# Three changes to one attention and mixer kernel: 64x64 float32 products on unpadded tiles, remainders in groups, attention tiles held to a clock

## The chip, the cores and the metric

The kernel runs on one core of one Trainium2 chip. The core has five engines that work through their own instruction lists in order: TensorE (PE in the rows; PEld is its weight load), VectorE (DVE), ScalarE (ACT), GpSimd (POOL) and SyncE (SP), which here only issues DMAs. The metric is the device time of one execution in microseconds; lower is better.

## The reference

```python
def _attn_ref(q, k, v):                     # B, H, S, D = 8, 8, 576, 64; chunks of 64 positions
    scores = scale * np.matmul(q_c, k_c.transpose(0, 1, 2, 4, 3))
    scores = scores - np.max(scores, axis=-1, keepdims=True)
    attn = np.exp(scores)
    attn = attn / (np.sum(attn, axis=-1, keepdims=True) + 1e-09)
    out = np.matmul(attn, v_c)

def _moe_ref(x, w_in, w_spatial, b_spatial, w_out):     # x: (8, 576, 512)
    h = np.maximum(x @ w_in, 0.0)
    u, v = (h[..., :d_ff // 2], h[..., d_ff // 2:])
    ...
    v_n = (v - mu) / np.sqrt(var + 1e-06)
    v_s = np.einsum('ts,bsd->btd', w_spatial, v_n) + b_spatial[None, :, None]
    return ((u * v_s) @ w_out).astype(np.float32)

def _moe2_ref(x, U, V, w_ch1, w_ch2):
    h = x.transpose(0, 2, 1) @ U @ V
    u = x + h.transpose(0, 2, 1)
    ch = np.maximum(u @ w_ch1, 0.0) @ w_ch2
    return (u + ch).astype(np.float32)
```

Attention works inside chunks of 64 positions, so each of the 8 x 8 x 9 chunks is a 64x64 score block of its own. Its output goes through the two mixers.

## The kernel before

**Tiles.** The host lays the attention inputs out as 36 tiles of 128x512: two chunks stacked on the partitions (rows 0 to 63 and 64 to 127), 8 heads of 64 columns. Tiles 0 to 8 belong to batch elements 0 and 1 (nine tiles for two elements; tile 4 holds the last chunk of both), and so on.

**Two ways to do attention.** Tiles 0 to 8 (`gen_first`) are multiplied in float32. A product uses the whole 128x128 array: the two chunks' q stand block-diagonally in a zero-padded 128x128 weight block `qb`, so one product per head gives both chunks' scores `sp` (L516), and likewise `vb` for the outputs `of` (L537). DVE and POOL write the zeros (L445 to L448), a DMA brings q and v to a staging place, and ACT copies the halves to their places (L478, L498); q of tiles 5 to 8 is loaded straight into place by two DMAs each (L487). Between the products are the maximum, subtraction, exponential, sum and division (`a_softmax`, `a_norm`) and a transpose `tp` on PE (L529). Tiles 9 to 35 (`gen_attn`) use three float16 products (`mm3`: high by high, high by low, low by high), for which ACT and POOL split q, k, v and the attention into a high and a low part (L362 to L366, L375, L376, L571, L572), in buffers that are written for each tile anew.

**Mixers.** `gen_moe(b)` does, for batch element b, the products `pb<-w,xT` with a layer norm (L655 to L631), `up` (L678), the spatial product with `sp_m` (L693 to L695, gated on DVE at L697), the product with `w_o`, a transposing DMA `tr`, and the rank-32 update: `u_stage` gives `ast`, `v_stage` multiplies it with `v4` (L746), adds it into `x2` on DVE (L747) and splits the sum into the slice buffer `uT` (ACT L750, POOL L751). The last stage cuts the 8 x 576 positions into 9 slices of 512; so element b's first `512 - 64*b` positions end slice b, and the remaining `64 + 64*b` begin slice b+1, one `v_stage` for each of the four 128-row groups m. `gen_ch(j)` does the two large products on slice j: `phid`, then `hid` (ACT L828, DVE L830), then `acc`, over 16 blocks f.

**Weights.** All weights arrive as float64 bit patterns. Each is converted by ACT (L173), three DVE steps (L180, L181, L184), ACT (L191) and POOL (L192) into a high and a low half. Twelve are needed for the first mixer, and 32 more (two for each f) for `gen_ch(0)`; `want(f)` makes sure that those of f stand ahead of its products. Weights and the q and k of tiles 9 on share three staging buffers (`ld4`).

**Order.** Tiles 0 to 4 come first, together with eight weights; then element 0's mixer, with tiles 5 to 8 and the start of element 1's in its gaps. After that three streams (attention from tile 9, mixers, `gen_ch`) are woven together by `Flow.run`, a planner with a clock of its own in ns: it takes from the first stream, in the order of priority, whose time has come. A scheduler then sets each engine's final order from its own estimate of times, so a change in one place moves instructions elsewhere. PSUM has few buffers: three (`h`) are shared by all `pb` and `phid`, and one (`a`) by the float16 scores, their outputs and the transposes.

```python
            if kind == "pe":
                self.tick(val)
                self.t += val
                best[1] = self.t + val * best[3]
            elif kind == "wait":
                best[1] = max(best[1], self.t + val)
```

Of the kernel before, what the change touches and what calls it, by code (L numbers as in the profile page):

```python
# [36 lines left out]
LDV = (3, 4)  # L37
MEMSET = (0, 1, 0, 1, 1)
# [14 lines left out]
class Flow:  # L53
# [13 lines left out]
    def run(self):  # L67
        while self.streams:
            best = None
            for s in self.streams:  # L70
                if s[2] is not None:
                    if s[2] in self.ev:
                        s[1] = max(s[1], self.ev[s[2]])
                        s[2] = None
                    else:
                        continue
                if s[1] <= self.t:
                    best = s
                    break
            if best is None:  # L80
                t = min(s[1] for s in self.streams if s[2] is None)
                self.t = t
                continue
            try:
                kind, val = next(best[0])
            except StopIteration:
                self.streams.remove(best)
                continue
# [5 lines that stand above are left out]
                best[1] = max(best[1], self.t + val)  # L94
            elif kind == "pace":
                best[3] = val
            elif kind == "need":
                best[2] = val
# [3 lines left out]
def moe_kernel(  # L102
# [46 lines left out]
    def mm3(o, wh, wl, xh, xl, start, stop):  # L149
        nc.tensor.matmul(out=o, lhsT=wh, rhs=xh, start=start, stop=False)  # L150
# [273 lines left out]
    def first_loads():  # L424
# [17 lines left out]
        for i in range(5):  # L442
            z = wf[:, i * 3072:i * 3072 + 2048]
            if i < 1:
                nc.vector.memset(z[:, 0:1024], 0.0)  # L445
                nc.gpsimd.memset(z[:, 1024:2048], 0.0)
            else:
                (nc.gpsimd if MEMSET[i] else nc.vector).memset(z, 0.0)  # L448
# [21 lines left out]
    def first_qk(i):  # L470
        qb, vb, kf, pt = first_bufs(i)
        if i < 5:
            qs = wf[:, 15360 + (i % 2) * 512:15360 + (i % 2 + 1) * 512]
            nc.sync.dma_start(out=qs, in_=q[i])
            nc.sync.dma_start(out=kf, in_=k[i])
            for c in range(2):
                r = slice(c * 64, (c + 1) * 64)
                nc.scalar.copy(out=qb[r, :, c, :], in_=qs[r].rearrange("p (h n) -> p h n", h=H))  # L478
            if i + 1 in FILL:

                z = idle[i + 1] = sb.tile([128, 512], F16, tag=("ph", "kd", "se")[i], name="idle", bufs=1 + (i == 2))
                nc.vector.memset(z, 0.0)
                nc.scalar.activation(out=z[0:1, 0:1], in_=qs[0:1, 0:1], func=ACTF.Copy, scale=0.0)
            return
        for c in range(2):
            r = slice(c * 64, (c + 1) * 64)
            nc.sync.dma_start(out=qb[r, :, c, :], in_=q[i][r].rearrange("p (h n) -> p h n", h=H))  # L487
        nc.sync.dma_start(out=kf, in_=k[i])

    def first_v(i):  # L490
        qb, vb, kf, pt = first_bufs(i)
        vs = pt.rearrange("p a n -> p (a n)")
        if i in LDV:
            vs = sb.tile([128, 512], F32, tag="ldv", name="vs", bufs=1)
        nc.sync.dma_start(out=vs, in_=v[i])
        for c in range(2):
            r = slice(c * 64, (c + 1) * 64)
            nc.scalar.copy(out=vb[r, :, :, c, :], in_=vs[r].rearrange("p (a c e) -> p a c e", a=4, c=2))  # L498

    def first_bufs(i):  # L500
        o = (0, 1, 2, 3, 4, 2, 3, 4, 2)[i] * 3072
        qb = wf[:, o:o + 1024].rearrange("p (h c n) -> p h c n", h=H, c=2)
        vb = wf[:, o + 1024:o + 2048].rearrange("p (a c x e) -> p a c x e", a=4, c=2, x=2)
        kf = wf[:, o + 2048:o + 2560]
        pt = wf[:, o + 2560:o + 3072].rearrange("p (a n) -> p a n", a=4)
        return qb, vb, kf, pt

    def gen_first(lo, hi):

        for i in range(lo, hi):  # L510
# [4 lines left out]
            for h in range(H):  # L515
                nc.tensor.matmul(  # L516
                    out=sp[:, h, :], lhsT=qb[:, h].rearrange("p c n -> p (c n)"), rhs=kf[:, h * 64:(h + 1) * 64],
                    start=True, stop=True,
                )
# [14 lines left out]
            for hp in range(4):  # L534
                for c in range(2):
                    tt = slice(c * 64, (c + 1) * 64)
                    nc.tensor.matmul(  # L537
                        out=o[:, hp, tt], lhsT=vb[:, hp, c].rearrange("p x e -> p (x e)"), rhs=pt[:, hp, tt],
                        start=True, stop=True,
                    )  # L540
# [6 lines left out]
    def gen_attn(lo, hi):  # L547
# [5 lines left out]
        for i in range(lo, hi):  # L553
# [3 lines left out]

            kd = spl.pop(i)
            sp = ps_a.tile([128, H, 64], F32, tag="a", name="sp")
            qm = qbd.rearrange("p a h c t -> p a h (c t)")  # L560
            for h in range(H):
                mm3(sp[:, h, :], qm[:, 0, h, :], qm[:, 1, h, :], kd[:, 0, h, :], kd[:, 1, h, :], True, True)
# [40 lines left out]
    def gen_moe(b):  # L603
# [191 lines left out]
        for m in range(4):  # L795
            v_stage(m, n1, S - n1, b + 1, 0)
            yield "pe", mmcost(S - n1)
# [201 lines left out]
```

## Time and profile before

| | |
|---|---|
| median of 3 runs (lowest, highest) | 1310.97 us (1307.9, 1312.58) |
| the profiled execution's own time | 1309.03 us |
| its span, first to last instruction | 1307.1 us |
| PE busy | 1261.7 us, 97% |
| DVE, ACT, POOL busy | 510.3, 518.2, 512.3 us |
| mean granted TensorE clock | 0.990 |

A busy time is the sum of the stretches in which an engine works. A matmul's end is modelled, and the next one starts before it ends, so PE's busy time says where PE stands still and not how full it is while it works. The profiled execution lies 1.94 us below the median.

### The profile page before, as it was taken

How to read it: one execution, taken by the hardware profiler on the slowest of the kernel's cores; microseconds unless marked ns; L12 is line 12 of the kernel's file. 1: busy time of each engine (PE TensorE's matmuls, PEld its weight loads, DVE VectorE, ACT ScalarE, POOL GpSimd, SP SyncE). 2: the span in 40 equal slices, each digit the busy share in tenths (PEclk: the TensorE clock that was granted, in tenths of full speed). 3: DMA queues.
4: the chain of work that ended last, by engine and by line, in shares of the span. 5: the costliest groups of instructions: out<-in, count | busy, mean ns of one | idle time of the engine just before them, and what ended most of it. 6: DMA issues, size and time to landing. Idle time of an engine off the chain costs nothing.

```text
span 1307.1 us, 20572 instructions
## 1 busy us (share of the span) xinstructions
PE 1261.7 (97%) x8324; PEld 722.9 (55%) x8324; DVE 510.3 (39%) x946; ACT 518.2 (40%) x1062; POOL 512.3 (39%) x644
## 2 busy tenths in 40 slices
PE   7899887899999999999999999999999999999998
PEld 5677455444666556654665456645654565544443
DVE  7965787655333533334233513242113211221211
ACT  7865566545445434534244424323123212221110
POOL 6755877646556444525155415223111311020000
PEclk7899899999999999999999999999999999999999
DMA  7645353532224311321034101300011001000000
GB/s 284 194 134 134 113 170 91 132 90 73 64 63 92 82 25 42 83 43 42 5 74 84 49 1 33 45 33 5 1 28 42 1 1 29 24 18 1 33 1 33
DMA packets 99015, 81.43 MB, mean 62 GB/s; under 512 B 73828, under 2 KB 74468, under 8 KB 98920
## 3 DMA queue, kind: packets, MB, share of 16 engines
q1 hardware_dynamic: 97768, 75.92, 21.8%
q10 hardware_dynamic: 1152, 4.19, 1.0%
q8 instruction: 65, 1.06, 0.3%
q14 instruction: 30, 0.25, 0.1%
HBM read 53.62 MB, written 9.44 MB: 48 GB/s over the span
## 4 chain that ended last, share of the span: by engine, by line
PE 79%; DVE 6%; DMA 4%; ACT 4%; POOL 4%; issue 2%; SPq 0%; DVEq 0%; ACTq 0%; POOLq 0%
PE acc L150 9%; PE acc L152 9%; PE acc L151 9%; PE phid L150 9%; PE phid L151 9%; PE phid L152 9%; PE pb L150 8%; PE pb L151 8%; PE pb L152 8%; DMA st<-in_wk_dram 2%; DVE dt L181 2%; DVE dt L184 2%; POOL wch L192 1%; ACT dt L173 1%; DVE dt L180 1%
## 5 line engine op out<-in xcount | busy, mean ns | idle before, releaser
L830 DVE SCALAR_TENSOR_TENSOR hid<-phid,hid 128x512 f16<-128x512 f32 x144 | 99.1, 690 | 388.3 <-ACT hid L828 388.2
L150 PE MATMUL phid<-uT,wch 128*128 128x512 f16 x576 | 218.8, 380 | 2.3 <-DVE hid L830 2.3
L151 PE MATMUL acc<-hid,wch 128*128 128x512 f16 x576 | 218.3, 379 | 0.8 <-DVE hid L830 0.8
L151 PE MATMUL phid<-uT,wch 128*128 128x512 f16 x576 | 218.6, 380 | 0.0
L152 PE MATMUL phid<-uT,wch 128*128 128x512 f16 x576 | 218.6, 379 | 0.0
L152 PE MATMUL acc<-hid,wch 128*128 128x512 f16 x576 | 218.3, 379 | 0.0
L150 PE MATMUL acc<-hid,wch 128*128 128x512 f16 x576 | 207.0, 379 | 0.5 <-ACT hid L828 0.4
L152 PEld LDWEIGHTS <-wch 128*128 128x128 f16 x1152 | 112.8, 98 | 132.8 <-issue 1.6
L150 PEld LDWEIGHTS <-wch 128*128 128x128 f16 x1152 | 112.8, 98 | 118.2 <-issue 2.4
L151 PEld LDWEIGHTS <-wch 128*128 128x128 f16 x1152 | 112.8, 98 | 117.3 <-issue 3.0
L828 ACT ACTIVATE hid<-phid 128x512 f16<-128x512 f32 x144 | 85.4, 595 | 189.8 <-PE phid L152 189.0
L376 POOL TENSOR_TENSOR vbd<-vf,vbd 64x512 f16<-64x512 f32 x54 | 64.6, 1197 | 112.1 <-ACT vbd L375 105.2
L702 POOL TENSOR_TENSOR gt<-g,gt 128x288 f16<-128x288 f32 x64 | 50.4, 789 | 142.4 <-ACT gt L700 142.1
L363 POOL TENSOR_TENSOR qbd<-qk,qbd 64x512 f16<-64x512 f32 x54 | 63.8, 1181 | 53.4 <-ACT qbd L362 51.4
L768 POOL TENSOR_TENSOR tr<-x,tr 128x64 f16<-128x64 f32 x64 | 46.8, 752 | 92.1 <-issue 50.0
L751 POOL TENSOR_TENSOR uT<-x,uT 128x512 f16<-128x512 f32 (+7 forms) x64 | 47.6, 755 | 89.0 <-ACT uT L750 86.1
L150 PE MATMUL pb<-xT,w 128*128 128x288 f16 x256 | 73.8, 288 | 2.3 <-DVE x L747 1.4
L150 PE MATMUL pb<-sp_m,vn 128*128 128x288 f16 x256 | 73.2, 286 | 2.8 <-DVE g L697 1.7
L150 PE MATMUL pb<-gt,w 128*128 128x288 f16 x256 | 72.9, 286 | 3.0 <-DVE hid L830 2.3
L152 PE MATMUL pb<-xT,w 128*128 128x288 f16 x256 | 73.8, 288 | 0.0
L151 PE MATMUL pb<-xT,w 128*128 128x288 f16 x256 | 73.8, 288 | 0.0
L152 PE MATMUL pb<-sp_m,vn 128*128 128x288 f16 x256 | 73.2, 286 | 0.0
(179 smaller groups left out, 2305.0 us busy)
## 6 DMA issues: line engine op xcount, KB each, us to landing
st<-in_wk_dram SPq DMA_DIRECT2D x24, 512.0 KB, 3.5
out_dram<-ot SPq DMA_DIRECT2D x32, 256.0 KB, 2.1
vf<-in_v_dram SPq DMA_DIRECT2D x27, 256.0 KB, 2.7
qk<-in_q_dram SPq DMA_DIRECT2D x27, 256.0 KB, 2.7
qk<-in_k_dram SPq DMA_DIRECT2D x27, 256.0 KB, 3.0
room<-in_wk_dram SPq DMA_DIRECT2D x8, 512.0 KB, 7.2
wch<-in_wk_dram ACTq DMA_DIRECT2D x8, 512.0 KB, 3.2
wch<-in_k_dram SPq DMA_DIRECT2D x9, 256.0 KB, 4.4
```

The lines of the kernel that those rows point to most:

```text
L150: nc.tensor.matmul(out=o, lhsT=wh, rhs=xh, start=start, stop=False)
L151: nc.tensor.matmul(out=o, lhsT=wh, rhs=xl, start=False, stop=False)
L152: nc.tensor.matmul(out=o, lhsT=wl, rhs=xh, start=False, stop=stop)
L181: nc.vector.scalar_tensor_tensor(out=tb, in0=w[:, 0::2], scalar=29, in1=tb, op0=ALU.logical_shift_right, op1=ALU.bitwise_or)
L184: nc.vector.scalar_tensor_tensor(out=tb, in0=w[:, 1::2], scalar=0x80000000, in1=tb, op0=ALU.bitwise_and, op1=ALU.bitwise_or)
L363: nc.gpsimd.tensor_tensor(out=qbd[r, 1, :, c, :], in0=qv[r], in1=qbd[r, 0, :, c, :], op=ALU.subtract)
L376: nc.gpsimd.tensor_tensor(out=vbd[r, 1, :, :, c, :], in0=vf[r], in1=vbd[r, 0, :, :, c, :], op=ALU.subtract)
L702: nc.gpsimd.tensor_tensor(out=gt[:, 1, m, c], in0=g, in1=gt[:, 0, m, c], op=ALU.subtract)
L751: nc.gpsimd.tensor_tensor(out=buf[:, 1, m, c], in0=x2[:, m, t], in1=buf[:, 0, m, c], op=ALU.subtract)
L768: nc.gpsimd.tensor_tensor(out=th[:, o0:o0 + n], in0=x2[:, m, t0:t0 + n], in1=th[:, t0:t0 + n], op=ALU.subtract)
L828: nc.scalar.activation(out=hd[:, 0, :], in_=p, func=ACTF.Relu)
L830: nc.vector.scalar_tensor_tensor(out=hd[:, 1, :], in0=p, scalar=0.0, in1=hd[:, 0, :], op0=ALU.max, op1=ALU.subtract)
```

## The change

For tiles 0 to 8 the zero padding, the staging and the copies go: q, k and v are loaded once, straight to where they are used, and every product is split in two products of 64x64, one for each chunk, on rows 0 to 63 and 64 to 127. The tiles' places in the buffer are listed in `FIRST_AT_COL`. In the mixer, the remainder `S - n1` of the four groups m is done `g = min(4, 512 // n2)` groups at a time in one PSUM buffer, with one DVE, one ACT and one POOL instruction for all of them. For tiles 9 to 17 the planner gets a new word, `until`: tile i isn't begun before 45000 + 16000 (i - 9) ns of its clock, and the first score product of these tiles is kept where the program puts it.

```diff
+FIRST_AT_COL = (0, 3072, 6144, 9216, 12288, 6144, 9216, 12288, 6144)
...
+            elif kind == "until":
+                best[1] = max(best[1], val)
...
+    def mm3(o, wh, wl, xh, xl, start, stop, pin=False):
+        m = nc.tensor.matmul(out=o, lhsT=wh, rhs=xh, start=start, stop=False)
+        if pin:
+            tc.keep_in_program_order(m)
...
-        for i in range(5):
-            z = wf[:, i * 3072:i * 3072 + 2048]
-            if i < 1:
-                nc.vector.memset(z[:, 0:1024], 0.0)
-                nc.gpsimd.memset(z[:, 1024:2048], 0.0)
-            else:
-                (nc.gpsimd if MEMSET[i] else nc.vector).memset(z, 0.0)
...
     def first_qk(i):
         qb, vb, kf, pt = first_bufs(i)
-        if i < 5:
-            qs = wf[:, 15360 + (i % 2) * 512:15360 + (i % 2 + 1) * 512]
-            nc.sync.dma_start(out=qs, in_=q[i])
-            nc.sync.dma_start(out=kf, in_=k[i])
-            for c in range(2):
-                r = slice(c * 64, (c + 1) * 64)
-                nc.scalar.copy(out=qb[r, :, c, :], in_=qs[r].rearrange("p (h n) -> p h n", h=H))
...
-        for c in range(2):
-            r = slice(c * 64, (c + 1) * 64)
-            nc.sync.dma_start(out=qb[r, :, c, :], in_=q[i][r].rearrange("p (h n) -> p h n", h=H))
+        nc.sync.dma_start(out=qb, in_=q[i])
         nc.sync.dma_start(out=kf, in_=k[i])
...
     def first_v(i):
-        qb, vb, kf, pt = first_bufs(i)
-        vs = pt.rearrange("p a n -> p (a n)")
...
-        nc.sync.dma_start(out=vs, in_=v[i])
-        for c in range(2):
-            r = slice(c * 64, (c + 1) * 64)
-            nc.scalar.copy(out=vb[r, :, :, c, :], in_=vs[r].rearrange("p (a c e) -> p a c e", a=4, c=2))
+        nc.sync.dma_start(out=first_bufs(i)[1], in_=v[i])
...
             for h in range(H):
-                nc.tensor.matmul(
-                    out=sp[:, h, :], lhsT=qb[:, h].rearrange("p c n -> p (c n)"), rhs=kf[:, h * 64:(h + 1) * 64],
-                    start=True, stop=True,
-                )
+                for c in range(2):
+                    r, n = slice(c * 64, (c + 1) * 64), slice(h * 64, (h + 1) * 64)
+                    nc.tensor.matmul(out=sp[r, h, :], lhsT=qb[r, n], rhs=kf[r, n], start=True, stop=True)
...
+                    for x in range(2):
+                        r = slice(x * 64, (x + 1) * 64)
+                        nc.tensor.matmul(
+                            out=o[r, hp, tt], lhsT=vb[r, hp * 128 + c * 64:hp * 128 + (c + 1) * 64], rhs=pt[r, hp, tt],
+                            start=True, stop=True,
+                        )
...
+            if i < 18:
+                yield "until", 45000.0 + 16000.0 * (i - 9)
...
-                mm3(sp[:, h, :], qm[:, 0, h, :], qm[:, 1, h, :], kd[:, 0, h, :], kd[:, 1, h, :], True, True)
+                mm3(sp[:, h, :], qm[:, 0, h, :], qm[:, 1, h, :], kd[:, 0, h, :], kd[:, 1, h, :], True, True,
+                    i < 18 and h == 0)
...
-        for m in range(4):
-            v_stage(m, n1, S - n1, b + 1, 0)
-            yield "pe", mmcost(S - n1)
+        n2 = S - n1
+        g = min(4, 512 // n2)
+        buf = slice_buf(b + 1)
+        for m0 in range(0, 4, g):
+            p = b_psum(b)
+            o = p[:, 0:g * n2].rearrange("p (m t) -> p m t", m=g)
+            for j in range(g):
+                nc.tensor.matmul(out=o[:, j], lhsT=ast[:, m0 + j, :], rhs=v4[:, n1:S], start=True, stop=True)
+            ms = slice(m0, m0 + g)
+            t = x2[:, ms, n1:S]
+            nc.vector.scalar_tensor_tensor(
+                out=t, in0=o, scalar=float(2 ** -14), in1=t, op0=ALU.mult, op1=ALU.add
+            )
+            nc.scalar.copy(out=buf[:, 0, ms, 0:n2], in_=t)
+            nc.gpsimd.tensor_tensor(out=buf[:, 1, ms, 0:n2], in0=t, in1=buf[:, 0, ms, 0:n2], op=ALU.subtract)
+            yield "pe", mmcost(n2, g)
```

The lines of the changed kernel are numbered a few lower or higher than before; in the excerpts below L494 is what L516 was, L504 what L529 was, L514 what L537 was, L183, L184 and L187 what L180, L181 and L184 were, L599 what L618 was, and L786 is the new DVE step of a grouped remainder.

First, PE's order right after the 16 fill products that stand ahead of tile 1's scores. `sp` are scores, `tp` transposes, `of` outputs of the float32 tiles, `pb<-w,xT` the first mixer. Before:

```order
L516 MATMUL sp<-wch 128x64 x8
L529 MATMUL tp<-ident,wch 128x128 x4
L537 MATMUL of<-wch 128x64 x8
L516 MATMUL sp<-wch 128x64 x8
L150 LDWEIGHTS xT
L150 MATMUL pb<-w_75,xT 128x512
```

and of the change:

```order
L494 MATMUL sp<-wch 64x64 x48
L504 MATMUL tp<-ident,wch 128x128 x4
L514 MATMUL of<-wch 64x64 x16
L151 LDWEIGHTS xT
L151 MATMUL pb<-w_75,xT 128x512
```

The scores of tiles 1, 2 and 3 now stand in one piece ahead of tile 0's transposes; before, it was tile 1's alone.

Second, DVE's order at the end of element 0's mixer, where the remainder of 64 positions is added into `x2`; `rz` and `mv` belong to element 1's layer norm, `dt` to weights. Before:

```order
L618 TENSOR_SCALAR rz_1427<-rz_1427,mv_1431,y_1434 128x512
L657 BN_AGGR mv_1488<-bs_1486 128x2
L181 SCALAR_TENSOR_TENSOR dt_1503<-st_1501,dt_1503 128x512
L747 SCALAR_TENSOR_TENSOR x2_1029<-pb_1557,x2_1029 128x64
L747 SCALAR_TENSOR_TENSOR x2_1029<-pb_1562,x2_1029 128x64
L659 TENSOR_SCALAR mv_1488<-mv_1488 128x1
L184 SCALAR_TENSOR_TENSOR dt_1503<-st_1501,dt_1503 128x512
L747 SCALAR_TENSOR_TENSOR x2_1029<-pb_1567,x2_1029 128x64
L747 SCALAR_TENSOR_TENSOR x2_1029<-pb_1572,x2_1029 128x64
```

and of the change:

```order
L638 BN_AGGR mv_1592<-bs_1590 128x2
L184 SCALAR_TENSOR_TENSOR dt_1607<-st_1605,dt_1607 128x512
L640 TENSOR_SCALAR mv_1592<-mv_1592 128x1
L786 SCALAR_TENSOR_TENSOR x2_1072<-pb_1661,x2_1072 128x4x64
L187 SCALAR_TENSOR_TENSOR dt_1607<-st_1605,dt_1607 128x512
L599 TENSOR_SCALAR rz_1531<-rz_1531,mv_1535,y_1538 128x512
```

Four steps in four PSUM buffers became one step in one buffer, and the normalisation of element 1's second row block, which waits for POOL, moved from ahead of the remainder to behind it.

Third, DVE's order around the last of the 32 weight conversions for `gen_ch(0)`; `mx` and `se` are an attention tile's maximum and scores. Before, the rows are those of tile 13:

```order
L385 TENSOR_REDUCE mx_2472<-sp_2447 128x8
L830 SCALAR_TENSOR_TENSOR hid_3144<-phid_3077,hid_3144 128x512
L184 SCALAR_TENSOR_TENSOR dt_2792<-st_2790,dt_2792 128x512
L388 TENSOR_TENSOR se_2474<-sp_2447,mx_2472 128x512
...
L397 TENSOR_TENSOR se_2474<-se_2474,sp_2447 128x512
L180 TENSOR_SCALAR dt_2827<-dt_2827 128x512
L747 SCALAR_TENSOR_TENSOR x2_2553<-pb_3147,x2_2553 128x448
L181 SCALAR_TENSOR_TENSOR dt_2827<-st_2825,dt_2827 128x512
L184 SCALAR_TENSOR_TENSOR dt_2827<-st_2825,dt_2827 128x512
```

and of the change, where the attention rows are those of tile 11:

```order
L183 TENSOR_SCALAR dt_2666<-dt_2666 128x512
L184 SCALAR_TENSOR_TENSOR dt_2666<-st_2664,dt_2666 128x512
L187 SCALAR_TENSOR_TENSOR dt_2666<-st_2664,dt_2666 128x512
L728 SCALAR_TENSOR_TENSOR x2_2299<-pb_2759,x2_2299 128x448
L414 TENSOR_TENSOR xT_2355<-o_2594,xT_2355 128x4x128
L716 SCALAR_TENSOR_TENSOR ast_2301<-pb_2744,ast_2301 32x128
L824 SCALAR_TENSOR_TENSOR hid_2784<-phid_2740,hid_2784 128x512
L388 TENSOR_REDUCE mx_2728<-sp_2703 128x8
```

Before, the softmax steps of five tiles (9 to 13) stood ahead of the last conversion; now it is two (9 and 10), and tile 11's first step stands behind it. On POOL the number of attention tiles whose q and k are split ahead of the last conversion falls from six to three.

## Rows read from the trace of the kernel before

**Rows 1.** Windows: stretch, length; busy us of PE, PEld, DVE, ACT, POOL; clock; DMA; GB/s.

```profile
0.00:20.00 20.00, 14.46 (x60) 7.43 (x61) 14.21 (x27) 13.88 (x24) 10.97 (x13) 0.83 0.90 333
20.00:60.00 40.00, 32.64 (x197) 25.90 (x197) 36.07 (x68) 33.02 (x58) 32.22 (x32) 0.83 0.69 212
60.00:87.00 27.00, 24.49 (x184) 18.65 (x184) 21.35 (x50) 19.80 (x46) 15.07 (x24) 1.00 0.45 147
87.00:146.00 59.00, 50.88 (x388) 37.78 (x388) 37.22 (x71) 34.20 (x81) 34.56 (x43) 0.96 0.44 117
146.00:272.00 126.00, 109.42 (x839) 64.56 (x837) 92.79 (x134) 74.47 (x163) 93.35 (x88) 0.99 0.47 130
272.00:1307.00 1035.00, 1029.79 (x6670) 568.61 (x6666) 308.62 (x600) 342.85 (x694) 326.13 (x446) 1.00 0.15 38
```

**Rows 2.** Timeline of DVE near its start: start us, us, instruction [idle before].

```profile
1.31 0.91 DVE L445 MEMSET wch<- 128x1024 f32 x1 [0.16 <-issue]
2.60 1.76 DVE L448 MEMSET wch<- 128x2048 f32 x1 [0.38 <-issue]
8.56 0.43 DVE L180 TENSOR_SCALAR dt<-dt 128x512 uint32<-128x512 uint32 x1 [4.19 <-ACT dt L173]
```

**Rows 3.** Groups of DVE up to 68 us: count, busy us, mean ns, idle before.

```profile
L181 DVE SCALAR_TENSOR_TENSOR dt<-st,dt 128x512 uint32<-128x512 uint32 x4 | 4.0, 993 | 0.0
L184 DVE SCALAR_TENSOR_TENSOR dt<-st,dt 128x512 uint32<-128x512 uint32 x4 | 3.7, 926 | 0.0
L394 DVE TENSOR_REDUCE sp<-wch 128x8 f32<-128x512 f32 x6 | 4.1, 681 | 0.0
```

**Rows 4.** Timeline, DVE and PE around the start of the spatial product.

```profile
67.82 0.68 DVE L418 TENSOR_TENSOR xd<-of,xd 128x512 f16<-128x512 f32 x1
83.04 0.55 DVE L618 TENSOR_SCALAR rz<-rz,mv,y 128x512 f32<-128x512 f32 x1 [0.64 <-POOL y L615]
86.91 0.28 PE L150 MATMUL pb<-sp_m,vn 128*128 128x288 f16 x1 [1.12 <-ACT up L678]
```

**Rows 5.** Groups of ACT over the whole execution, the copies of q and v.

```profile
L478 ACT COPY wch<-wch 64x512 f32<-64x512 f32 x10 | 6.2, 616 | 1.4 <-DMA wch<-in_q_dram 1.3
L498 ACT COPY wch<-wch 64x512 f32<-64x512 f32 x14 | 8.6, 615 | 2.2 <-DMA wch<-in_v_dram 2.1
```

**Rows 6.** Timeline of PE and PEld: float32 products, then float16 products of tile 16.

```profile
6.08 1.97 PEld L516 LDWEIGHTS sp<-wch 128*128 128x128 f32 x16
6.29 1.89 PE L516 MATMUL sp<-wch 128*128 128x64 f32 x16
12.52 6.40 PE L465 MATMUL sp<-idle 128*128 128x512 f16 x16 [4.34 <-ACT idle L483]
320.96 0.19 PE L150 MATMUL sp<-kd,qbd 128*128 128x64 f16 x1
320.99 0.19 PE L151 MATMUL sp<-kd,qbd 128*128 128x64 f16 x1
```

**Rows 7.** Timeline where element 0's remainder is added.

```profile
139.26 1.37 DVE L618 TENSOR_SCALAR rz<-rz,mv,y 128x512 f32<-128x512 f32 x1
141.49 0.34 PE L746 MATMUL pb<-v,ast 128*128 128x64 f16 x2 [4.07 <-DVE x L747]
143.25 0.40 PE L150 MATMUL pb<-xT,w 128*128 128x288 f16 x1 [1.42 <-DVE x L747]
```

**Rows 8.** Groups of POOL from 146 to 272 us.

```profile
L192 POOL TENSOR_TENSOR wch<-dt,wch 128x512 f16<-128x512 f32 x24 | 30.1, 1254 | 20.7 <-ACT wch L191 20.6
L363 POOL TENSOR_TENSOR qbd<-qk,qbd 64x512 f16<-64x512 f32 x10 | 12.9, 1293 | 5.5 <-ACT qbd L362 5.1
L376 POOL TENSOR_TENSOR vbd<-vf,vbd 64x512 f16<-64x512 f32 x8 | 10.5, 1309 | 2.6 <-ACT vbd L375 2.3
L366 POOL TENSOR_TENSOR kd<-qk,kd 128x512 f16<-128x512 f32 x6 | 7.5, 1256 | 0.3
L572 POOL TENSOR_TENSOR ph<-se,ph 128x512 f16<-128x512 f32 x5 | 6.7, 1335 | 1.4 <-ACT ph L571 1.4
```

More of the change, by code (lines that the diff above doesn't have):

```diff
@@ L36 @@
 SP_AFTER = 5
-LDV = (3, 4)
-MEMSET = (0, 1, 0, 1, 1)
+FIRST_AT_COL = (0, 3072, 6144, 9216, 12288, 6144, 9216, 12288, 6144)
 WA, WB, WC = 2500.0, 5500.0, 2500.0
@@ L147, in moe_kernel @@
     fl = Flow()
-    def mm3(o, wh, wl, xh, xl, start, stop):
-        nc.tensor.matmul(out=o, lhsT=wh, rhs=xh, start=start, stop=False)
+    def mm3(o, wh, wl, xh, xl, start, stop, pin=False):
+        m = nc.tensor.matmul(out=o, lhsT=wh, rhs=xh, start=start, stop=False)
+        if pin:
+            tc.keep_in_program_order(m)
         nc.tensor.matmul(out=o, lhsT=wh, rhs=xl, start=False, stop=False)
@@ L471, in first_qk @@
         qb, vb, kf, pt = first_bufs(i)
-        if i < 5:
-            qs = wf[:, 15360 + (i % 2) * 512:15360 + (i % 2 + 1) * 512]
-            nc.sync.dma_start(out=qs, in_=q[i])
-            nc.sync.dma_start(out=kf, in_=k[i])
-            for c in range(2):
-                r = slice(c * 64, (c + 1) * 64)
-                nc.scalar.copy(out=qb[r, :, c, :], in_=qs[r].rearrange("p (h n) -> p h n", h=H))
[L479 to L484, printed above, removed]
-        for c in range(2):
-            r = slice(c * 64, (c + 1) * 64)
-            nc.sync.dma_start(out=qb[r, :, c, :], in_=q[i][r].rearrange("p (h n) -> p h n", h=H))
+        nc.sync.dma_start(out=qb, in_=q[i])
         nc.sync.dma_start(out=kf, in_=k[i])
+        if i + 1 in FILL:
+            z = idle[i + 1] = sb.tile([128, 512], F16, tag=("ph", "kd", "se")[i], name="idle", bufs=1 + (i == 2))
+            nc.vector.memset(z, 0.0)
+            nc.scalar.activation(out=z[0:1, 0:1], in_=qb[0:1, 0:1], func=ACTF.Copy, scale=0.0)
     def first_v(i):
-        qb, vb, kf, pt = first_bufs(i)
-        vs = pt.rearrange("p a n -> p (a n)")
-        if i in LDV:
-            vs = sb.tile([128, 512], F32, tag="ldv", name="vs", bufs=1)
-        nc.sync.dma_start(out=vs, in_=v[i])
-        for c in range(2):
-            r = slice(c * 64, (c + 1) * 64)
-            nc.scalar.copy(out=vb[r, :, :, c, :], in_=vs[r].rearrange("p (a c e) -> p a c e", a=4, c=2))
-    def first_bufs(i):
[L501 to L506, printed above, removed]
+        nc.sync.dma_start(out=first_bufs(i)[1], in_=v[i])
+    def first_bufs(i):
+        o = FIRST_AT_COL[i]
+        return [wf[:, o + j * 512:o + (j + 1) * 512] for j in range(3)] + [
+            wf[:, o + 1536:o + 2048].rearrange("p (a n) -> p a n", a=4)]
     def gen_first(lo, hi):
@@ L536, in gen_first @@
                     tt = slice(c * 64, (c + 1) * 64)
[L537 to L540, printed above, removed]
+                    for x in range(2):
[4 more added lines that the diff above has]
+                        )
             a_out(i, o)
@@ L556, in gen_attn @@
             a_load(i + 1)
+            if i < 18:
+                yield "until", 45000.0 + 16000.0 * (i - 9)
             kd = spl.pop(i)
+            pin = True
             sp = ps_a.tile([128, H, 64], F32, tag="a", name="sp")
```

## The prediction

> **What bounds the kernel now.** I read the page's first part, then the windows view by stages, then the waits, the timeline and the groups of the stages in which PE stands still. Columns of rows 1 after the length are PE, PEld, DVE, ACT and POOL. From 272 us to the end PE is busy 1029.79 of 1035 us [rows 1]; DVE, ACT and POOL are at about 30% there. What is done to those three engines in that stretch costs or gives nothing; only PE's own work counts. Before 272 us PE stands still for 5.54, 7.36, 2.51, 8.12 and 16.58 us in the five stages, 40.1 in all, and the granted clock is 0.83 up to 60 us [rows 1]. So the change can win from three places: those 40 us, the half-speed stretches among them, and PE's work on float32 products.
>
> Who holds PE up? From 20 to 60 us DVE is busy 36.07 of 40 us [rows 1]: it makes the softmax of tiles 0 to 4 and three of the six engine steps of each weight conversion, and PE gets its tiles at DVE's pace. From 146 to 272 us DVE is busy 92.8 and POOL 93.4 of 126 us [rows 1], in order and interlocked with ACT: PE waits there in many pieces, and the conversions of the 32 late weights share the engines with the attention of tiles 9 to 13. Between, the largest piece is one place: 4.07 and 1.42 us at the remainder of element 0 [rows 7].
>
> **Term 1, up to 87 us: 5 us less.** ACT loses 24 copies of q and v, 10 x 0.616 + 14 x 0.615 = 14.8 us [rows 5]. ACT is busy 66.7 of the first 87 us, so this shortens its queue, but it isn't the tightest engine. DVE is. It loses two memsets of 0.91 and 1.76 us, which are worth nothing: DVE then waits 4.19 us for the first weight anyway [rows 2]. POOL's memsets precede its first subtraction and hide in the same way. More comes from the order: ahead of L418, the last step of tile 4, stand 113 DVE instructions before and 93 now. Of the 20, two are the memsets (2.7 us), six are tile 5's softmax (four passes of 0.68 [rows 3] and two short ones, 3.1), the rest are ten steps of conversions and two of u, at most 0.99 each [rows 3], of which some are on 160 or 288 columns; I take 7. That is 12.8, less the 2.7: 10 us less DVE work. Against it: the maximum of tile 1 now stands ahead of tile 0's last multiplication on DVE and must wait for the 16 fill products (12.52 to 18.92) and tile 1's scores [rows 6]; I count 2 us. So L418, at 67.82 [rows 4], would come some 8 us sooner. The spatial product starts at 86.91, some 3.9 us after the last L618 [rows 4]; ahead of that one DVE row list shrinks by only 12 (143 to 131), some 9 us by the same prices, less 2.7 and 2: 4 to 5. PE itself needs, after L418, 12 products at 0.22, 96 at 0.12 and two float32 groups, 18 us, so it doesn't forbid that. I take 5, between 0 (the order only shuffles what DVE must do) and 10.
>
> **Term 2, the remainder at 137 to 146 us: 6 us less.** Four remainders need four of the three shared PSUM buffers, and DVE frees the first only after L618, which itself took 1.37 us while waiting [rows 7]. Now one buffer and one DVE step hold all four, and the L618 stands behind it. The 5.5 us of waiting go, and with them most of the half-speed stretch that follows (0.96 of 59 us [rows 1] is 2.4 us). DVE, ACT and POOL do one step of 256 columns for four of 64, no dearer. I take 6, from 0 (PE waits for the next DVE step in line) to 8. At elements 1 to 7 PE is full and nothing shows.
>
> **Term 3, 146 to 272 us: 11 us less.** With `until`, two attention tiles instead of five stand ahead of the last conversion on DVE, and three instead of six on POOL. A tile costs POOL two L363, two L376, one L366 and one L572: 2 x 1.29 + 2 x 1.31 + 1.26 + 1.34 = 7.8 us [rows 8]; three tiles are 23 of its 93 us. DVE loses three times five passes of 0.68 and two short steps, 11 us of 93. ACT loses as much as POOL or more. The same conversions then need 82 us of DVE and 70 of POOL while PE has 109.4 us of work there, so no engine but PE is near its limit. Of the 16.58 us of standing still I take two thirds, 11; the ends are 0 and 16.6. The three tiles aren't saved, they come later; after 272 us DVE and POOL have 70% free, which hides them. If that cover were gone, they would cost what they cost now.
>
> **Term 4, float32 products: 0, from 7 less to 24 more.** Eight products of 128x64 are 16 PE instructions, started 0.11 us apart (1.89 us less the last one's 0.2, over 15), and their weight loads are as far apart [rows 6]: the load of 128 float32 columns sets the pace. A new tile has 32 instructions for scores and 32 for outputs, each with 64 columns of weights. No row shows such a product. Lower end: 0.03 us each, as the float16 products with 64 moving columns [rows 6]. Upper end: 0.11, if the load of a quarter takes as long. Half the columns at the same rate is 0.056, and 32 x 0.056 = 1.8 us, what 16 x 0.11 is now; I take that, since half of the nearest row's load is half of its columns. There are 18 groups. At 0.03 they would be 15 us shorter, about half of it (8 groups after 60 us) on the path: 7. At 0.11 they would be 18 x 32 x 0.055 = 32 us longer; the first ten groups lie in the 60 us where PE stands still for 12.9, so some 24 stay.
>
> The Trainium skill (TensorE: Matmul & The Clock Gate, the section on LDWEIGHTS) puts the load in proportion to the columns, 53 ns for 64 as an estimate; by that the sum is the same. It isn't shown by a row here.
>
> **Term 5, changes of shape: 3 us more, from 0 to 7.** The new products form 22 separate pieces in PE's order, so 44 changes between 64x64 and 128x128. A float16 product lasts 0.19 us from start to end while the next starts 0.03 later [rows 6]. If PE must run empty at each change, that is 0.16 x 44 = 7 us; if not, nothing. About half of the pieces lie where PE stands still anyway; I take 3.
>
> The Trainium skill (TensorEngine Tiling (Array Packing), Key Properties) says that a change of the tiling mode, as against a change of the tile, drains TensorE. That rule speaks against this change; by it alone the upper end, 7, would hold and the sum would be 1294. No row here shows it, so it has four chances in ten inside the forecast's own case.
>
> **Sum.** The profiled execution took 1309.03 us, 1.94 below the median. 1309.0 - 5 - 6 - 11 + 0 + 3 = 1290.0 us. The PE work behind 272 us stays.
>
> **Rivals.**
> - *Pairs overlap.* The two 64x64 products use different rows and columns of the array. If they run side by side, term 4 is at its lower end and the time is 1283; if PE's waiting also shrinks more than by two thirds, down to 1270. For it: that the two need different parts of the array; against it: the rows show only whole-array products, one after the other. Chance 0.17. The Trainium skill (TensorE: Matmul & The Clock Gate, Part 3 on packing small matmuls) has weight loads overlap running products when the row groups differ; no run here shows it yet.
> - *The gains move.* The delayed tiles collide with the next mixer, or DVE, still full from 20 to 60 us, gives term 1 nothing, and PE waits elsewhere. Terms 2 and 3 at a third: 1309 - 6 + 3 = 1306; with nothing at all 1309. For it: DVE's work is nearly the same. Against: DVE is at 30% after 272 us. Chance 0.13.
> - *Slower.* A 64-column load costs as much as a 128-column load. With the other terms halved, 1309 - 11 + 3 + 24 = 1325; with all of them, 1314. It decides from about 0.10 us an instruction on: there term 4 eats the 19 us of the rest. For it: the pace is set by the load, and its floor for small loads isn't shown. Against: the float16 products start 0.03 us apart, so nothing on PE forces 0.11 for each instruction. Chance 0.11.
>
> **Numbers.** The forecast's own case, 1279 to 1302, has 0.59. Below 1270 I leave about 0.07, above 1307 about 0.13, so the range is 1270 to 1307. One run is told from another at about 0.3%, 4 us: faster 0.81, same 0.08 (most of the second rival's milder half), slower 0.11.
>
> **What would show it.** Right: PE busy from about 255 us on without gaps; the spatial product starting near 82 us; no wait of PE for the grouped DVE step above 1 us; new scores taking 1.8 us a tile; PE's standing still before 272 us near 18 us in place of 40. Wrong: float32 groups of 3.6 us or of 0.9; PE waiting after 272 us for `xT`, which would mean that tiles 9 to 17 come too late; DVE's L418 still at 67 us.

## The result, and the profile of the changed kernel

| | before | after |
|---|---|---|
| median of 5 runs, us | 1311.81 (1307.9 to 1312.58) | 1298.71 (1297.43 to 1299.04) |
| ratio, 95% interval | | 0.991 [0.9893, 0.9927] |
| profiled execution: span | 1307.1 | 1296.9 |
| PE busy / DVE / ACT / POOL | 1261.7 / 510.3 / 518.2 / 512.3 | 1251.6 / 507.3 / 500.2 / 504.5 |

The change makes the kernel 13.1 us faster by the medians, 11.8 by the ratio, and 10.3 between the two profiled executions (1309.03 and 1298.71). The forecast took its 19 us from 1309.0, and its 1290.0 lies 8.7 us below the time. The windows view of the changed kernel, cut as in [rows 1] (columns: stretch, its length, then busy time of PE, PEld, DVE, ACT, POOL, granted clock, DMA share, GB/s):

```profile
0.00:20.00 20.00, 14.25 (x162) 7.83 (x163) 12.88 (x27) 7.36 (x12) 5.01 (x10) 1.00 0.94 344
20.00:60.00 40.00, 29.95 (x310) 18.37 (x308) 34.04 (x62) 27.68 (x49) 31.81 (x32) 0.74 0.64 221
60.00:87.00 27.00, 24.10 (x187) 16.63 (x188) 26.70 (x57) 17.74 (x43) 15.80 (x24) 0.87 0.43 131
87.00:146.00 59.00, 52.17 (x504) 35.67 (x503) 36.10 (x65) 32.30 (x76) 39.58 (x49) 1.00 0.45 124
146.00:272.00 126.00, 112.98 (x793) 65.83 (x792) 85.12 (x131) 70.30 (x153) 79.83 (x72) 0.97 0.45 121
272.00:1297.00 1025.00, 1018.19 (x6662) 564.38 (x6660) 312.44 (x596) 344.83 (x693) 332.43 (x445) 1.00 0.15 39
```

Subtract PE's busy time from each length, and PE stands still for 5.75, 10.05, 2.90, 6.83 and 13.02 us up to 272 us. That is 38.6 us in all, where it was 40.1. So the time that was to vanish is nearly all still there, and PE's busy time fell by 10.1 us, as much as the span. Nor did the stretches of lower granted clock go: what its column lacks of 1.00, times the lengths up to 272 us, is some 13.8 us before and 17.7 now, an estimate from these rows. Read alone, the two numbers of PE say that the shorter float32 products made the gain. The experiments will show that this reading is wrong.

The timeline of the changed kernel at the places that the prediction named (start, duration, engine, line, what; in brackets the idle time before it and what ended it):

```profile
7.33 1.15 PE L494 MATMUL sp<-wch 64*64 64x64 f32 x32
19.81 0.83 PE L504 MATMUL tp<-ident,wch 128*128 128x128 f32 x4 [2.10 <-DVE wch L400]
35.01 0.62 ACT L194 CAST w<-dt 128x512 f16<-128x512 f32 x1 [3.00 <-DVE dt L187]
36.16 1.97 PE L514 MATMUL of<-wch 64*64 64x64 f32 x32 [4.50 <-ACT wch L505]
61.58 0.68 DVE L421 TENSOR_TENSOR xd<-of,xd 128x512 f16<-128x512 f32 x1
81.72 0.28 PE L151 MATMUL pb<-sp_m,vn 128*128 128x288 f16 x1 [0.58 <-ACT up L659]
134.41 0.28 PE L783 MATMUL pb<-v,ast 128*128 128x64 f16 x4
136.75 0.38 PE L151 MATMUL phid<-uT,wch 128*128 128x512 f16 x1 [0.59 <-DVE x L786]
```

Three things stand there. A float32 group of 32 instructions lasts 1.15 us, not 1.8 (1.97 at 36.16, in a stretch whose granted clock is 0.74 on the mean). DVE's last step of tile 4 (L421, L418 before) starts at 61.58 instead of 67.82, and the spatial product at 81.72 instead of 86.91 [rows 4]. The four remainders are one piece of 0.28 us, and what follows waits 0.59 us for their one DVE step instead of 4.07 and 1.42 [rows 7]. But there are new waits at the start. PE waits 4.50 us for ACT's copy L505, because ACT, working in order, stood 3.00 us at a weight's cast (L194) that waits for DVE. The longest groups of PE's waits (total, times, longest):

```profile
PE of L514 <- ACT wch L505: 6.2, 3, 4.5
PE pb L711 <- DMA tr<-tr: 4.4, 3, 2.1
PE o L151 <- DMA pt<-ph: 3.1, 2, 2.8
PE pb L155 <- DVE xd L421: 2.9, 1, 2.9
```

The POOL subtractions of the 32 late weights, one line of the view by source line (count, minimum/median/maximum in ns, first and last start), end much sooner than the 272 us of before:

```profile
L195 POOL TENSOR_TENSOR wch<-dt,wch x32: 1146/1158/1624, 83.3 to 240.6; 128x512 f16<-128x512 f32 x32
```

### The profile page after: what moved, and what is told of

Same layout as the page of the kernel before. It is cut to its first block, busy times and chain, and to the rows that moved or that the text cites. A ratio compares the mean times of both kernels' runs of the same rounds, so it can differ in the third digit from the quotient of the medians.

```text
span 1296.9 us, 21079 instructions
## 1 busy us (share of the span) xinstructions
PE 1251.6 (97%) x8612; PEld 708.7 (55%) x8612; DVE 507.3 (39%) x934; ACT 500.2 (39%) x1024; POOL 504.5 (39%) x630
## 4 chain that ended last, share of the span: by engine, by line
PE 80%; DVE 7%; DMA 5%; POOL 4%; ACT 2%; issue 2%; SPq 0%; DVEq 0%; POOLq 0%; ACTq 0%
PE acc L151 9%; PE phid L151 9%; PE phid L155 9%; PE phid L154 9%; PE acc L155 9%; PE acc L154 9%; PE pb L151 7%; PE pb L155 7%; PE pb L154 7%; DVE dt L184 2%; DVE dt L187 2%; DMA wch<-in_q_dram 1%; DMA tr<-tr 1%; DVE dt L183 1%; POOL wch L195 1%
## 5 line engine op out<-in xcount | busy, mean ns | idle before, releaser
L151 PE MATMUL pb<-sp_m,vn 128*128 128x288 f16 x256 | 73.2, 286 | 2.8 <-DVE hid L824 1.5
L154 PE MATMUL pb<-gt,w 128*128 128x288 f16 x256 | 73.7, 288 | 2.1 <-POOL gt L683 2.1
L151 PE MATMUL pb<-gt,w 128*128 128x288 f16 x256 | 73.5, 288 | 1.8 <-ACT tr L746 1.7
L155 PE MATMUL pb<-gt,w 128*128 128x288 f16 x256 | 73.6, 288 | 0.0
```

What stands on the lines that cost most here:

```text
L151: m = nc.tensor.matmul(out=o, lhsT=wh, rhs=xh, start=start, stop=False)
L154: nc.tensor.matmul(out=o, lhsT=wh, rhs=xl, start=False, stop=False)
L155: nc.tensor.matmul(out=o, lhsT=wl, rhs=xh, start=False, stop=stop)
```

## Experiments

Twelve kernels, each run 4 to 12 times beside the kernel before. The intervals reach 1.4 to 2.8 us to each side, so a difference of under some 3 us between two kernels is uncertain. "Last conversion" is the start of the last POOL subtraction in the view just shown; in the kernel before it is 270.8 us.

| kernel | median us | ratio to before, 95% | last conversion, us |
|---|---|---|---|
| clock alone | 1304.73 | 0.9956 [0.9939, 0.9972] | 244.8 |
| float32 part alone | 1307.95 | 0.9979 [0.9966, 0.9993] | 260.5 |
| grouping alone | 1312.0 | 1.0004 [0.999, 1.0018] | 269.3 |
| change without grouping | 1301.82 | 0.9934 [0.9918, 0.9951] | 242.3 |
| change without clock | 1307.94 | 0.9981 [0.997, 0.9992] | 268.6 |
| change, neighbours on the same rows | 1300.87 | 0.9921 [0.9905, 0.9937] | 242.9 |
| change, 24 idle products more | 1300.11 | 0.9922 [0.9904, 0.994] | 241.4 |
| change, clock 20 us earlier | 1306.51 | 0.9954 [0.9938, 0.997] | 244.3 |
| change, clock 10 us later | 1299.24 | 0.99 [0.9882, 0.9918] | 238.0 |
| change, clock 20 us later | 1307.24 | 0.9973 [0.9961, 0.9984] | 235.4 |
| change, clock 40 us later | 1314.49 | 1.0026 [1.0014, 1.0038] | 231.9 |
| change, late weights without sign | 1284.91 | 0.9793 [0.9772, 0.9814] | 221.9 |

**1. The change without the clock.** The first theory, M, took the profile at its word: the waits moved, and float32 pairs, start and remainder made the gain. Its rival C gave the gain to the clock.

```
-            if i < 18:
-                yield "until", 45000.0 + 16000.0 * (i - 9)
...
-                    i < 18 and h == 0)
+                    False)
```

> The changed kernel without the clock: tiles 9 to 17 yield no due time and their first score product is not held in program order; the rest of the change stays. Theory M (the waits of 146 to 272 us only moved, and the gain comes from side-by-side float32 pairs, the start and the remainder): about 1300 us, between 1297 and 1303, PE standing still before 272 us again 36 to 42 us. Theory C (the clock gave its forecast 11 us and something else took them back): 1308 to 1312.

Measured: 1307.94 us, 9.2 us more than with the clock, just under theory C's 1308. M falls. Without the clock the rest of the change is worth 0.19%, 2.5 us. Windows of this kernel, cut at 82, 140 and 300 us:

```profile
0.00:82.00 82.00, 62.82 (x620) 38.89 (x621) 68.56 (x135) 48.75 (x95) 51.92 (x63) 0.85 0.64 225
82.00:140.00 58.00, 52.62 (x505) 36.62 (x504) 39.91 (x73) 32.74 (x76) 34.27 (x41) 0.97 0.44 123
140.00:300.00 160.00, 141.19 (x1047) 80.54 (x1046) 112.94 (x162) 89.27 (x192) 108.21 (x99) 0.97 0.42 120
```

The same cut of the changed kernel:

```profile
0.00:82.00 82.00, 63.30 (x617) 38.89 (x618) 68.80 (x134) 49.05 (x95) 51.36 (x63) 0.83 0.65 224
82.00:140.00 58.00, 51.90 (x510) 36.19 (x508) 39.89 (x73) 33.59 (x77) 35.40 (x42) 1.00 0.46 126
140.00:300.00 160.00, 146.25 (x1015) 83.06 (x1015) 101.67 (x162) 85.41 (x182) 98.11 (x101) 0.98 0.41 114
```

And of the kernel before:

```profile
0.00:82.00 82.00, 67.71 (x405) 48.69 (x406) 70.09 (x141) 63.34 (x119) 54.90 (x64) 0.88 0.69 227
82.00:140.00 58.00, 51.67 (x407) 39.14 (x406) 34.27 (x63) 32.73 (x75) 33.09 (x43) 1.00 0.44 115
140.00:300.00 160.00, 140.51 (x1058) 80.68 (x1058) 110.49 (x170) 90.38 (x194) 107.44 (x101) 0.98 0.42 120
```

From 140 to 300 us PE stands still for 19.5 us before, 18.8 without the clock and 13.8 with it; DVE and POOL have 10 to 11 us less to do there with it than without. These 5.0 us are about half of the 9.2; the granted clock of the stretch, 0.98 instead of 0.97, is by 160 x 0.01 an estimated 1.6 more, and the rest isn't placed. Up to 82 us it stands still for 14.3 us before and for 19.2 and 18.7 with the new float32 products. There DVE's 69 to 70 busy us hardly differ, and what PE no longer needs for its products it waits.

The later runs test theory W, made from this: the last weight conversion ends the stretch in which PE stands still, so PE time won ahead of it is mostly waited out, and attention tiles ahead of it cost. Its rivals: P, that PE's own work decides; L, that delayed tiles come too late for element 2's mixer.

**2. The clock alone on the kernel before.** The same two edits, none of the others.

> The kernel before with the clock alone (due times and the held first product for tiles 9 to 17). Theory M: 1308 to 1313 us, no measurable difference. Theory C: 1298 to 1302 us.

1304.73 us: 0.44% or 5.8 us, between the theories. The clock is a gain by itself, but it gives more beside the rest of the change (9.2 us).

**3. The change without grouping, and 4. grouping alone.** The loop over four remainders in place of the grouped step, and the reverse.

```
-            for j in range(g):
-                nc.tensor.matmul(out=o[:, j], lhsT=ast[:, m0 + j, :], rhs=v4[:, n1:S], start=True, stop=True)
...
+        for m in range(4):
+            v_stage(m, n1, S - n1, b + 1, 0)
+            yield "pe", mmcost(S - n1)
```

> The changed kernel with the remainders one by one, as before. Both theories take the forecast's term 2 as right in size: 1303 to 1306 us, with a wait of some 4 us of PE for the second remainder's DVE step near 130 us. If the four remainders cost nothing now because DVE is less behind there: 1298 to 1300.

> The kernel before with grouped remainders alone. The forecast's term 2 by itself: 1303 to 1306 us. Theory W: the wait near 139 us goes, the last conversion does not move, and PE waits as much longer behind 146 us: 1309 to 1312.

Taken from the change, grouping is worth 3.1 us, between the two expectations; the slowest run with it (1299.04) is faster than the fastest without (1300.15). In place of the one wait of some 4 us stand two, and the channel mixer's first product (`phid`) starts at 141.45 instead of 136.75 us:

```profile
136.52 0.32 PE L727 MATMUL pb<-v,ast 128*128 128x64 f16 x2 [1.91 <-DVE x L728]
138.62 0.40 PE L151 MATMUL pb<-xT,w 128*128 128x288 f16 x1 [1.78 <-DVE x L728]
141.45 0.48 PE L151 MATMUL phid<-uT,wch 128*128 128x512 f16 x1
```

Put into the kernel before it is worth nothing: 1.0004. There, too, the channel mixer starts sooner; the kernel before, then the one with grouping:

```profile
146.08 0.63 PE L150 MATMUL phid<-uT,wch 128*128 128x512 f16 x1
140.75 0.38 PE L150 MATMUL phid<-uT,wch 128*128 128x512 f16 x1 [2.83 <-DVE mv L659]
```

But the last conversion starts at 269.3 instead of 270.8 us, and the 5.3 us are lost again behind it. That PE waits them out is shown only in part: from 140 to 300 us it stands still for 20.1 us instead of 19.5, at a granted clock of 0.97 instead of 0.98.

**5. The float32 part alone.** Neither grouping nor clock.

> The change's first part alone: 64x64 float32 products on operands loaded directly; remainders one by one and no clock. Theory W: what PE gains before 140 us it loses again waiting for the last conversion, 1308 to 1311 us, though the spatial product starts 5 us earlier than before. Rival P (PE's own sum decides, and the shorter float32 groups and the earlier start are kept): 1303 to 1306.

1307.95 us, 3.0 us less than the kernel before beside it: at theory W's edge, and short of rival P's 1303 to 1306. With grouping added (experiment 1) the channel mixer starts 3.3 us sooner (137.66 instead of 140.93), and the time is the same, 1307.94.

**6. Neighbours on the same rows.** The same 64x64 products, all on rows 0 to 63 first.

```
-            for h in range(H):
-                for c in range(2):
+            for c in range(2):
+                for h in range(H):
```

(and `x` outermost in the outputs' loop)

> The changed kernel with the same 64x64 products in another order: first all those on rows 0 to 63, then all those on rows 64 to 127, so that neighbours share their rows. Theory M (two products on different rows run side by side): 32 instructions take 1.8 us (0.056 each) or more instead of 1.15; at 1.8 us the time is about 1305 us, at 3.6 us (0.11 each) about 1320. If the 0.034 us comes from the small load alone and not from pairs: 1.15 us a group again and 1298 to 1300 us.

Timeline of this kernel:

```profile
6.62 1.90 PE L494 MATMUL sp<-wch 64*64 64x64 f32 x32
16.57 4.91 PE L494 MATMUL sp<-wch 64*64 64x64 f32 x96
```

1.90 us a group: about 0.058 us from start to start, when neighbours share their rows (and so their columns too). On different rows 32 take 1.15 us from the first start to the last end. So pairs do run side by side here. In time this is worth 1.4 us by the ratios and 2.2 by the medians, at the edge of what the runs can tell, and the expected 1305 us did not come, though PE has some 18 x 0.75 = 13 us more to do. It stands still that much less, 10.7 and 2.4 us in this kernel's first two windows, where the change has 18.7 and 6.1:

```profile
0.00:82.00 82.00, 71.27 (x608) 47.86 (x609) 68.20 (x133) 48.31 (x93) 49.97 (x63) 0.85 0.66 224
82.00:140.00 58.00, 55.59 (x509) 40.38 (x509) 40.12 (x73) 32.44 (x76) 34.30 (x41) 0.97 0.44 123
```

**7. Idle products.** 24 products of 512 columns ahead of tile 7's scores (they use the zeros made for tile 1's).

```
-FILL = {1: 16}
+FILL = {1: 16, 7: 24}
```

> The changed kernel with 24 more idle products of 512 columns, 24 x 0.216 = 5.2 us of PE, ahead of tile 7's scores near 110 us. Theory W: the last conversion moves little and most of the 5.2 us disappears in PE's waits before 242 us: 1299 to 1301. Rival P: 1303 to 1304.

1300.11 us: 5.2 us of PE work cost 1.4, inside theory W's range, and the last conversion starts at 241.4 instead of 240.6. One window of it:

```profile
140.00:300.00 160.00, 148.38 (x1036) 83.64 (x1035) 107.26 (x165) 87.33 (x185) 98.67 (x101) 1.00 0.40 115
```

PE stands still for 11.6 us there instead of 13.8. But the granted clock is 1.00 instead of 0.98 as well, by 160 x 0.02 an estimated 3 us, so only a part of the 5.2 us is shown to have gone into waits; whether the idle products kept the clock up isn't shown.

**8. Late weights without the sign step on DVE.**

```
+        if not (isinstance(name, int) and name >= 12):
             nc.vector.scalar_tensor_tensor(
                 out=tb, in0=w[:, 1::2], scalar=0x80000000, in1=tb, op0=ALU.bitwise_and, op1=ALU.bitwise_or
```

> The changed kernel with one DVE step less, the sign's, in the conversion of the 32 late weights (all their values become positive; this part of the computation is left out): 32 steps of 0.7 to 1.5 us less on DVE, 23 of them after 142 us. Theory W: the conversions pace PE from 142 to 242 us; their end comes 10 to 20 us earlier, PE's waiting there falls from 17 to under 10 us, 1288 to 1293 us. Rival: PE waits there for steps that no conversion holds up (hid, tr, pt): 1296 to 1299.

1284.91 us, 13.8 us less than the changed kernel and more than expected. One window of it:

```profile
140.00:300.00 160.00, 156.71 (x1116) 89.36 (x1116) 89.75 (x159) 92.96 (x196) 100.34 (x114) 1.00 0.41 117
```

PE stands still for 3.3 us there in place of 13.8, the granted clock is 1.00 instead of 0.98 (an estimated 3 us), and the last conversion starts at 221.9. So the conversions' DVE steps hold PE up, though none of its waits in this stretch of the changed kernel names a conversion: they stand in the same in-order list of DVE as steps that PE waits for. DVE has 11.9 us less to do there than in the change (89.75 and 101.67). No run took other work alone off DVE, so it isn't shown whether the conversions' end counts or DVE's load as such.

**9 to 12. The clock moved.** Only the 45000.0 in `until` differs: 25000, 55000, 65000, 85000.

> The changed kernel with the due times 20 us earlier: three attention tiles ahead of the last weight conversion instead of two. Theory W+L (each tile ahead of the last conversion costs about 3 us, (1307.9 - 1298.7) / 3, and later tiles are good only until element 2's mixer wants them, near 305 us): about 1302 us, last conversion's end near 250 us. If the clock's gain came from another place than the tiles' count: 1298 to 1300.

> The due times 10 us later: one tile and a part of the second ahead of the last conversion. Theory W+L: tile 13 is then done some 10 us later than in the changed kernel, about at the moment when element 2's mixer wants it; the gain of 1 to 3 us before 240 us and a new wait of 0 to 4 us near 305 us, together 1296 to 1301. A version that beats the changed kernel, if there is one, lies here.

> The changed kernel with every due time of the clock 20 us later: one attention tile instead of two ahead of the last weight conversion on POOL (five without the clock). Theory W (the last weight conversion ends the stretch in which PE stands still, so each tile ahead of it costs PE 2.5 to 3 us, a third of the 9.2 us that three tiles cost when the clock was taken away): about 1296 us. Rival L (the first tiles come too late for element 2's mixer): 1299 or more, with PE waiting for xT after 272 us.

> The same with the due times 40 us later: no attention tile ahead of the last conversion. Theory W: about 1293 us, and the last conversion's end near 225 us instead of 242. Rival L: 1299 to 1310, PE waiting for xT of tiles 18 on; the gain per tile also ends if PE has less work to put beside the conversions: 1297 to 1299.

10 us later is the same as the change (0.99 against 0.991); no version here beats it except the one that leaves work out. 20 us earlier costs 7.8 us by the medians and 5.8 by the ratios, two to two and a half times what "3 us a tile" gave: both expectations missed, and that linear price fell. The last conversion starts only 3.7 us later there; the window from 140 to 300 us has 18.1 us of standing still instead of 13.8. 20 and 40 us later the conversions do end sooner, but the time rises by 8.5 and 15.8 us. Rival L holds, with another wait than the `xT` it named. With the clock 20 us later PE stands still for 10.8 us from 140 to 300 us, 2.9 less than in the change, but then for 9.2 of 30 us, at a lower granted clock, where the change has no gap:

```profile
300.00:330.00 30.00, 20.76 (x162) 11.76 (x159) 13.38 (x27) 13.02 (x24) 16.69 (x24) 0.83 0.22 62
```

The timeline there, where tile 13 is due:

```profile
305.03 0.62 ACT L392 ACTIVATE se<-se 128x512 f32<-128x512 f32 x1
309.07 1.15 POOL L553 TENSOR_TENSOR ph<-se,ph 128x512 f16<-128x512 f32 x1
310.25 1.25 SPq L555 DMA_TRANSPOSE pt<-ph  x1
313.44 0.21 PE L151 MATMUL o<-pt,vbd 128*128 128x64 f16 x1 [8.04 <-DMA pt<-ph]
316.07 0.61 PE L151 MATMUL pb<-w,xd 128*128 128x512 f16 x1 [1.19 <-ACT xd L420]
```

The mixer of element 2 wants tile 13's `xd` at once (last row). PE waits 8.04 us through tile 13's whole chain, softmax on DVE and ACT, subtraction on POOL, transpose by DMA.

So theory W holds in part. Less work on DVE from 140 to 300 us lets PE go on (experiments 1 and 8), and PE time won or spent ahead of that stretch doesn't come out in full (3 to 7). But the start of the last conversion doesn't set the time: 260.5 and 268.6 go with the same 1307.9 us (experiments 5 and 1), and 242.3 and 244.3 with 1301.8 and 1306.5 (3 and 9).

## Why the prediction was right, and which terms were off

The time, 1298.71, lies inside the range and inside the forecast's own case. The sum was 19 us, counted from 1309.0; measured were 10.3 from there, and 13.1 by the medians. The largest term was right in kind, and it and term 2 were too large; the own case, 23 us wide, held the difference. By its steps:

- **Term 3, the clock: 11 forecast.** It is worth 9.2 us taken away from the change and 5.8 put into the kernel before. The mechanism held: with three attention tiles fewer ahead of it the last conversion starts 28 us sooner (240.6 against 268.6), and PE stands still less from 140 to 300 us. Experiment 8 shows that the conversions' DVE steps pace PE there. The size was too large by 2 to 5 us: DVE and POOL are still busy for 85.1 and 79.8 us from 146 to 272 us, not 82 and 70, and PE stands still for 13.0 us there, not 5.6. The sign "PE busy from about 255 us on without gaps" came true up to 300 us (17.00 of 17 and 28.00 of 28 us in windows from 255 and from 272); some waits, the longest 0.99 us, turned up later.
- **Term 2, the remainder: 6 forecast, 3.1 measured, and nothing without the clock.** This is the worst-sized term. The wait did go, and with it the lower granted clock behind it (1.00 from 87 to 146 us instead of 0.96): the first product of the channel mixer starts 9.3 us sooner (136.75 against 146.08), and 4.7 of that are gone without grouping. But as experiments 3 to 5 show, PE time won ahead of 146 us counts only in part: 4.7 us there are 3.1 at the end, and 5.3 and 3.3 are nothing. The prediction added the terms as if each were paid in full at the end.
- **Terms 1, 4 and 5: 2 us forecast together, 3.0 measured** (experiment 5 against before), 2.9 between experiments 2 and 3. Term 1's 5 us are exact at their place (5.2 at the spatial start). Since PE waited on from there, it isn't shown how much of them reached the end; the direct loads were not tried without the 64x64 products.
- **Term 4 and the rival "Pairs overlap".** The half-of-the-load price, 0.056 us, is what neighbours on the same rows cost (0.058); on different rows the lower end, 0.03, holds. So the rival named the mechanism, and its price of 7 us was wrong: experiment 6 gives 1.4 to 2.2 us. Half of the groups, it said, lie on the path. But up to 82 us PE stands still for 18.7 us with the shorter products where it stood for 14.3, and with the longer products of experiment 6 for 10.7. So most of what the pairs save there is waited.
- **Term 5, changes of shape: 3 us.** A 64x64 piece between other products costs, at full clock, 0.22 us from the last start ahead of it instead of 0.12, and 0.15 from its own last start to the next product where it is 0.03 within:

```profile
73.56 0.29 PE L155 MATMUL pb<-xT,w 128*128 128x288 f16 x1
73.78 0.33 PE L494 MATMUL sp<-wch 64*64 64x64 f32 x4
74.04 0.30 PE L151 MATMUL pb<-xT,w 128*128 128x288 f16 x1
```

  That is 0.1 + 0.12 us for each of 22 pieces, 4.8 us of PE at most. The number format isn't the reason for the way in: in the kernel before, a 128x128 float32 piece starts 0.12 us after the same kind of product:

```profile
73.18 0.29 PE L152 MATMUL pb<-xT,w 128*128 128x288 f16 x1
73.30 1.23 PE L537 MATMUL of<-wch 128*128 128x64 f32 x10
```

  The Trainium skill's rule that a change of mode drains TensorE (TensorEngine Tiling (Array Packing), Key Properties) agrees, at 0.11 us a change, two thirds of the 0.16 that the prediction's upper end took.
- **"PE's standing still before 272 us near 18 us in place of 40": wrong, it is 38.6.** 5.7 us less from 140 to 300 us met 4.4 us more up to 82 us. This sum can't judge the change: a busy us that moves into a wait leaves the end where it was. It also goes with the granted clock of the execution: with the clock of tiles 9 to 17 10 us later, PE stands still for 22.9 us up to 82 us at a granted clock of 0.90, where the change has 18.7 at 0.83, and the time is the same.
- **"The gains move"** was partly true. The waits that took over are DVE's and ACT's at the start (2.10, 4.50 and 2.9 us), not the next mixer: that collision shows only with the clock 20 or 40 us later.

The clock gives 5.8 us on the kernel before and 6.1 on the float32 part alone (1307.95 against 1301.82); it gives 9.2 only where the grouping is in, and grouping gives 3.1 only where the clock is in. So these 3 us are one gain of the two together, and 9.2 + 3.1 + 3.0 counts it twice. Left open: why the two need each other (the clock with grouping alone was not run); whether the due times or the held first product do the clock's work (never tried apart); and why one attention tile more, 20 us earlier, costs 5.8 to 7.8 us.

## What to carry to other kernels

Find the engine whose list sets the pace of a stage (here DVE with the conversions), and count time won on PE ahead of it in full only if that stage ends sooner too; put 5 us of idle work in, see how much comes out, and look at the granted clock before you put the rest down to waits. Don't attribute a gain by comparing sums of busy and idle time: here PE's busy time fell by the whole gain, and undoing that fall (experiment 6) cost some 2 us. Work that can move behind such a stage has a deadline from its next reader, so try the position on both sides.

## What the runs showed of the hardware

Two float32 products on different 64-row parts and different 64-column parts of the array overlapped: 32 instructions in 0.93 us from first to last start, against 0.058 us from start to start when neighbours shared both. And one and the same DVE step of a conversion takes very different times in one run of the changed kernel. By the view of source lines:

```profile
L187 DVE SCALAR_TENSOR_TENSOR dt<-wch,dt x12: 685/1161/1546, 157.9 to 198.7; 128x512 uint32<-128x512 uint32 x12
```

The timeline of two such steps, each with the POOL subtraction beside it:

```profile
157.94 1.53 DVE L187 SCALAR_TENSOR_TENSOR dt<-wch,dt 128x512 uint32<-128x512 uint32 x1
157.57 1.35 POOL L195 TENSOR_TENSOR wch<-dt,wch 128x512 f16<-128x512 f32 x1 [1.28 <-ACT wch L194]
164.44 0.69 DVE L187 SCALAR_TENSOR_TENSOR dt<-wch,dt 128x512 uint32<-128x512 uint32 x1
164.53 1.61 POOL L195 TENSOR_TENSOR wch<-dt,wch 128x512 f16<-128x512 f32 x1 [3.18 <-ACT wch L194]
```

In the first pair POOL started 0.37 us ahead, and the DVE step ended 0.55 us after POOL's end. In the second DVE started first, took 0.69 us, and POOL's subtraction took 1.61 instead of 1.16 and ended 1.01 us after DVE's end. Of the 44 such steps on 512 columns 20 took 0.92 us or more, and every one of them had a POOL instruction that began ahead of it, and ended 0.55 us after that one's end; of the 24 shorter ones 7 began beside a POOL instruction, with at most 0.17 us of it left. In these rows the later of the two waits for the earlier to end. The Trainium skill (SBUF — State Buffer, the section on two separate sides) says that these two engines share a pair of ports as an exclusive lock, which a DVE step with two inputs in SBUF, as this one, needs against a GpSimd instruction that reads SBUF, and that the one that comes second waits for the whole instruction; the four rows agree. It gives one reason why taking work from either engine between 146 and 272 us helps the other; no run separated it.
